# Order of the links of the down phase, and of two kinds of side work, in a fused attention and two-layer SiLU kernel

## The chip, the cores and the metric

The kernel runs on one core of a Trainium2 chip. The metric is the device time of one execution in microseconds (us), the median of several; lower is better. Engines are named as in the profile: PE (TensorE matmuls), PEld (TensorE weight loads), DVE (VectorE), ACT (ScalarE), POOL (GpSimd) and SP (SyncE, which issues nearly all DMAs).

## The reference

Three stages follow each other: an attention with a decay bias, a gated layer and a plain SiLU layer. The change lies in the last one, `_moe2_ref`, whose input is the 2304 x 512 result of the gated layer.

```python
def _moe_ref(x, w_gate, w_val, w_out):
    g = x @ w_gate
    silu = g * (1.0 / (1.0 + np.exp(-g)))
    val = x @ w_val
    return (silu * val @ w_out).astype(np.float32)

def _moe2_ref(x, w_in, w_out):            # x 2304 x 512, w_in 512 x 2048, w_out 2048 x 512
    h = x @ w_in
    g = h * (1.0 / (1.0 + np.exp(-h)))
    return (g @ w_out).astype(np.float32)

def reference(**kwargs):
    ...
    attn_out = _attn_ref(**attn_kwargs)
    B, H, S, D = attn_out.shape
    x = np.ascontiguousarray(attn_out.transpose(0, 2, 1, 3)).reshape(B * S, H * D)
    x = _moe_ref(x=x, **moe_kwargs)
    return _moe2_ref(x=x, **moe2_kwargs)
```

## The kernel before

**Matmuls in three parts.** Every fp32 operand is kept as a high part and a low part. A product is three matmuls: weight high by data high (L677 in the down phase), weight high by data low (L678), weight low by data high (L679). The up phase has L632, L635 and L636 for the same three. The high part of an intermediate is made by ACT (a copy, L112) and its low part by POOL (a subtraction, L609); the two together are `h_cut`. So L677 of a block needs ACT alone, and L678 behind it needs POOL.

**The last layer** runs from about 656 us to the end. Its tokens are taken in 3 groups of 768 (two halves of 384), its 2048 hidden columns in 8 pieces of 256, which makes 24 steps. Two steps, a = 2q and b = 2q + 1, and a down phase make a round q, 0 to 11; rounds 0 to 3 work on the first group of tokens, 4 to 7 on the second, 8 to 11 on the third. Both matrix products are written with seven block products in place of eight, so that sums and differences of blocks are operands too.

- `up2(i)` does the seven products of a step (the list UP, positions `("u", i, 0)` to `("u", i, 6)`), six matmuls each, into four PSUM banks of the pool `ps_m`. What comes out is made into SiLU values u0 to u3 and their differences t1 to t4.
- `down2(q)` does 14 links, `("d", q, 0)` to `("d", q, 13)`: the seven products X1 to X4, Y1, Y2, Z1, each once for step a (`e` = 0) and once for step b (`e` = 1). Each link is six matmuls, two output banks (m = 0, 1) by three. Chain X adds all its products up in the same two banks, chain Y in two others (pool `ps_o`), chain Z in two banks of `ps_m`. After each link of step b, DVE reads the chain's two banks into accumulators in SBUF (L114 the first time, L688 after it), and the next product of that chain may write them again only then. The operands are: X1 takes B11 (cut of u0), Y1 T1, X2 T2, Y2 B22 (cut of u3), X3 T3, Z1 B21 (cut of u2), X4 T4. X1, Z1 and X4 use one weight tile, named C; Y1, X2, X3 and Y2 another, named E.

**What sets the order.** All engines run in the order in which the code is written. `LINKS` gives the order of the links. `fill` is a table of side work: after position `at` of an up or down phase, the functions put there are written, on whichever engine they use. In it stand the `h_cut` of step a (in the up phase of b) and of step b (in the down phase), the differences `h_sub` on DVE (L614), the weight loads `u_load` on SP (L599), and the preparation of the next group's tokens: `x2_load` (L555) fetches them, `x2_sub` (L586) makes four differences t1 to t4 of them on DVE, in two halves each, and `x2_cut` makes the parts for matmuls on ACT (L112) and POOL (L565).

Of the kernel before, what the change touches and what calls it, by code (L numbers as in the profile page):

```python
# [43 lines left out]
    "Y1": ("T1", "E", 0, (1, 1)), "Y2": ("B22", "E", 3, (0, 1)), "Z1": ("B21", "C", 1, (0, 0)),  # L44
}
LINKS = [
    ("X1", 0), ("Y1", 0), ("X1", 1), ("Y1", 1), ("X2", 0), ("X2", 1), ("Y2", 0),
    ("Y2", 1), ("X3", 0), ("X3", 1), ("Z1", 0), ("Z1", 1), ("X4", 0), ("X4", 1),
]
CLOSED = ("Z1", "Y2", "X3", "X4")  # L50

# [15 lines left out]
def kernel(  # L67
# [42 lines left out]
    def copy(eng, out, in_, scale=1.0):  # L110
        if eng == "a":
            act_last[:] = [nc.scalar.activation(out=out, in_=in_, func=AF.Copy, scale=scale).ins]  # L112
        elif eng == "v":
            nc.vector.tensor_scalar(out=out, in0=in_, scalar1=scale, scalar2=None, op0=ALU.mult)  # L114
        else:
            nc.gpsimd.tensor_scalar(out=out, in0=in_, scalar1=scale, scalar2=1.0, op0=ALU.mult, op1=ALU.mult)
# [434 lines left out]
    def x2_load(t):  # L551
        for i in range(2):
            r = p2["x2", i] = p2["x2r"].tile([P, 2, 2, TN], F32, tag="x2r", name="x2r")
            src = x2_d[2 * i : 2 * i + 2, :, 2 * t * TN : 2 * (t + 1) * TN]
            nc.sync.dma_start(out=r, in_=src.rearrange("k p (h n) -> p k h n", h=2))  # L555
# [4 lines left out]
    def x2_cut(t, i, src=None, eng=nc.vector):  # L560
        x = p2["x", t, i] = p2["x2"].tile([P, 2, 2, TN], F32R, tag="x2", name="x2")
        if src is None:
            src = p2["x2", min(i, 1)][:, :, {0: 0, 2: 0, 5: 1}[i]]
        copy("a", x[:, 0], src)
        eng.tensor_tensor(out=x[:, 1], in0=src, in1=x[:, 0].bitcast(F32), op=ALU.subtract)  # L565

    def x2_sub(t, k, halves=(0, 1)):
        u, d = p2["x2", 0], p2["x2", 1]
        if 0 in halves:
            if t > 0:  # L570
                o = {1: None, 2: None, 3: u[:, :, 1], 4: u[:, :, 0]}[k]
                if o is None:
                    o = p2["st"].tile([P, 2 * TN], F32, tag="st", name="stage").rearrange("p (k n) -> p k n", k=2)
            else:
                if k % 2:
                    p2["tt"] = p2["x2"].tile([P, 2, 2, TN], F32, tag="x2", name="tt")
                o = p2["tt"][:, (k + 1) % 2]
            p2["t", k] = o
        a, b = {
            1: (u[:, :, 1], u[:, :, 0]), 2: (d[:, :, 1], p2.get(("t", 1))),  # L580
            3: (d[:, :, 1], u[:, :, 1]), 4: (d[:, :, 0], p2.get(("t", 2))),
        }[k]
        o = p2["t", k]
        if len(halves) == 1:
            o, a, b = [x[:, halves[0]] for x in (o, a, b)]
        nc.vector.tensor_tensor(out=o, in0=a, in1=b, op=ALU.subtract)  # L586

    def u_load(i, names):
        for name in names:
            wide = 768 if name in "ZC" else CW // 2  # L590
            if (i, name) == (1, "Z"):
                w = p2["x2"].tile([P, 2, wide], F32R, tag="x2", name="z1")
            elif name in "ZC" and i > 0 or name == "C":
                w = p2["wt2"].tile([P, 2, wide], F32R, tag="wt2", name="wt2")
            else:
                w = p2["wt"].tile([P, 2, CW // 2], F32R, tag="wt", name="wt")
            p2["w", i, name] = w
            src = wu_d[steps[i][1], "ZSCE".index(name), :, :, :wide]
            nc.sync.dma_start(out=w[:, :, :wide].bitcast(F32), in_=src)  # L599

    def part(i, name):
        p2["u", i, name] = p2["tmp"].tile([P, TN], F32, tag=name + str(i % 2) * (name in ("t3", "t4")), name=name)
        return p2["u", i, name]

    def h_cut(i, name, src):
        h = hs["2", i, name] = p2["h"].tile([P, 2, TN], F32R, tag="h2", name="h2")
        u = p2["u", i, src]
        copy("a", h[:, 0], u)
        nc.gpsimd.tensor_tensor(out=h[:, 1], in0=u, in1=h[:, 0].bitcast(F32), op=ALU.subtract)  # L609

    def h_sub(i, out, a, b):
        x, y = p2["u", i, a], p2["u", i, b]
        o = p2["u", i, out] if ("u", i, out) in p2 else part(i, out)
        nc.vector.tensor_tensor(out=o, in0=x, in1=y, op=ALU.subtract)  # L614
# [164 lines left out]
    def body():  # L779
# [57 lines left out]
        for c in range(last):  # L837
            b = batch[c]
            cur = chunk_steps(c)
            at = {k: [] for k in range(5)}  # L840
            if b + 1 < B:
                k, u0 = c % len(L1), (b + 1) * H
# [35 lines left out]
        for c in range(last, n1):  # L878
            cur = chunk_steps(c)
            k = c - last  # L880
# [4 lines left out]
            i = tail_pieces.get(c)  # L885
# [51 lines left out]
        def put(at, *f):  # L937
            fill.setdefault(at, []).extend(f)

        nq = len(steps) // 2  # L940
        for q in range(nq):
            a, b = 2 * q, 2 * q + 1
            put(("u", b, 0), lambda i=a: h_cut(i, "T1", "t1"), lambda i=a: h_cut(i, "T3", "t3"))
            put(("u", b, 0), lambda i=a: h_sub(i, "t2", "u3", "t1"))
            put(("u", b, 1), lambda i=a: h_cut(i, "B21", "u2"), lambda i=a: h_sub(i, "t4", "u2", "t2"))
            put(("u", b, 2), lambda i=a: h_cut(i, "T2", "t2"))
            put(("u", b, 6), lambda i=b: h_sub(i, "t2", "u3", "t1"), lambda i=a: h_cut(i, "T4", "t4"))
            put(("d", q, 0), lambda i=b: h_cut(i, "T1", "t1"), lambda i=b: h_sub(i, "t4", "u2", "t2"))
            put(("d", q, 1), lambda i=b: h_cut(i, "T2", "t2"))
            put(("d", q, 2), lambda i=b: h_cut(i, "T3", "t3"))  # L950
            put(("d", q, 3), lambda i=b: h_cut(i, "B21", "u2"))
            put(("d", q, 4), lambda i=b: h_cut(i, "T4", "t4"))
            if q > 0:
                put(("u", a, 0), lambda a=a: (u_load(a, "C"), u_load(a + 1, "C")))
                put(("u", a, 3), lambda a=a: (u_load(a, "E"), u_load(a + 1, "E")))
            else:
                put(("u", b, 0), lambda: u_load(1, "E"))
            if q + 1 < nq:
                put(("u", b, 1), lambda a=a: u_load(a + 2, "ZS"))
                put(("d", q, 0), lambda a=a: u_load(a + 3, "ZS"))  # L960
        for t in range(1, TG):
            q = 4 * t - 1
            put(("u", 2 * q - 5, 2), lambda t=t: x2_load(t))
            for at, x in (
                ((q - 1, 6), 0), ((q - 1, 7), 3), ((q - 1, 9), 1), ((q, 6), 4), ((q, 7), 2), ((q, 8), 5), ((q, 9), 6),
            ):
                src = {1: 1, 3: 2, 4: 3, 6: 4}.get(x)
                put(("d", *at), lambda t=t, x=x, k=src: x2_cut(t, x, p2["t", k] if k else None, nc.gpsimd))
            for e in range(2):
                for at, k in ((q - 3, 4), 1), ((q - 2, 4), 2), ((q - 1, 4), 3), ((q - 1, 10), 4):  # L970
                    put(("d", at[0], at[1] + 2 * e), lambda t=t, k=k, e=e: x2_sub(t, k, (e,)))
        for q in range(nq):
            up2(2 * q, fill)
# [3 lines left out]
        second_layer.close()  # L977

    body()


# [42 lines left out]
```

## Time and profile before

| | |
|---|---|
| median of 3 runs | 1030.31 us (1029.67 to 1032.68) |
| the profiled execution's own time | 1030.3 us |
| its span, first to last instruction | 1028.5 us |
| mean granted TensorE clock | 0.993 |
| busy in the span | PE 97%, PEld 90%, POOL 57%, DVE 57%, ACT 51% |
| DMA | 260 GB/s on average |

The time is device time, the span is what the trace covers; 1.8 us lie outside it. Busy shares are means over all stages. Matmuls overlap each other in the trace (in the last layer one lasts about 0.34 us and the next starts some 0.175 us after it), so a busy PE says less than the distance from one matmul's start to the next.

### The profile page before, as it was taken

Reading aid. Unit: us, or ns where it says so; the run is one execution under the profiler, and the core shown is the slowest. Engines: PE = TensorE matmul, PEld = TensorE weight load, DVE = VectorE, ACT = ScalarE, POOL = GpSimd, SP = SyncE. Lnnn points to the kernel's source line nnn. Section 1 sums busy time; section 2 is a strip of 40 time slices with the busy share of each in tenths; the row PEclk is TensorE's granted clock in tenths of the full one; section 3 lists DMA queues with packets and bytes.
Section 4 is the critical chain, followed back from the end, with each engine's and each line's share of the span. In section 5 each row is a group of like instructions: output and inputs, shape, how many; then the busy total and the mean of one; then the engine's idle time right before and its main releaser. Section 6 shows DMA issues by size and latency. Waiting matters only on the chain.

```text
span 1028.5 us, 19469 instructions
## 1 busy us (share of the span) xinstructions
PE 996.6 (97%) x6864; PEld 930.2 (90%) x6864; DVE 584.7 (57%) x1492; ACT 523.7 (51%) x1230; POOL 589.8 (57%) x757
## 2 busy tenths in 40 slices
PE   8789999999999999999999999999999999999998
PEld 5468898899898899899899999999999999999997
DVE  5877768635745645545632223356665657555555
ACT  6868878625665435655533543323554234544232
POOL 4767656615866646757542765435766447764445
PEclk8989999999999999999999999999999999999999
DMA  8679798758789799766767767885777855786652
GB/s 234 175 240 309 262 326 255 265 174 269 261 295 267 258 311 305 276 230 238 273 221 278 292 262 286 319 330 225 277 286 282 301 212 216 290 317 244 237 203 94
DMA packets 81617, 267.16 MB, mean 260 GB/s; under 512 B 9904, under 2 KB 29360, under 8 KB 66160
## 3 DMA queue, kind: packets, MB, share of 16 engines
q1 hardware_dynamic: 81376, 265.73, 74.1%
q8 instruction: 54, 0.88, 0.3%
q14 instruction: 43, 0.35, 0.1%
q10 hardware_dynamic: 144, 0.20, 0.1%
HBM read 208.15 MB, written 57.75 MB: 259 GB/s over the span
## 4 chain that ended last, share of the span: by engine, by line
PE 75%; POOL 6%; ACT 3%; DVE 3%; DMA 2%; issue 2%; POOLq 0%; SPq 0%; DVEq 0%; ACTq 0%
PE pgv L490 9%; PE pgv L492 9%; PE pgv L491 9%; POOL h L609 6%; PE po L490 5%; PE po L491 5%; PE po L492 5%; PE po L678 5%; PE po L679 4%; PE po L677 4%; PE pv L324 4%; PE pu L636 3%; PE pu L632 3%; PE pu L635 3%; PE psc L213 3%; PE ptr L283 3%
## 5 line engine op out<-in xcount | busy, mean ns | idle before, releaser
L490 PE MATMUL pgv<-xt,wt 128*128 128x288 f32 x768 | 229.5, 299 | 1.9 <-DVE wraw L388 1.9
L492 PE MATMUL pgv<-xt,wt 128*128 128x288 f32 x768 | 226.3, 295 | 0.0
L491 PE MATMUL pgv<-xt,wt 128*128 128x288 f32 x768 | 226.1, 294 | 0.0
L609 POOL TENSOR_TENSOR h<-u,h 128x384 fp32r<-128x384 f32 x72 | 74.5, 1034 | 156.4 <-ACT h L112 152.1
L490 PEld LDWEIGHTS pgv<-xt,wt 128*128 128x128 f32 x768 | 144.2, 188 | 12.8 <-DVE m L230 5.9
L492 PEld LDWEIGHTS pgv<-xt,wt 128*128 128x128 f32 x768 | 144.0, 188 | 0.2 <-issue 0.2
L491 PEld LDWEIGHTS pgv<-xt,wt 128*128 128x128 f32 x768 | 144.1, 188 | 0.0
L504 POOL TENSOR_TENSOR h<-u,h 128x288 fp32r<-128x288 f32 x96 | 79.5, 830 | 88.2 <-ACT h L112 84.3
L112 ACT ACTIVATE h<-u 128x288 fp32r<-128x288 f32 (+1 forms) x168 | 79.7, 475 | 97.8 <-DVE u L502 96.8
L678 PE MATMUL po<-h,wt 128*128 128x384 f32 x336 | 113.8, 339 | 10.5 <-POOL h L609 10.5
L490 PE MATMUL po<-h,wt 128*128 128x288 f32 x384 | 114.8, 299 | 0.0
L677 PE MATMUL po<-h,wt 128*128 128x384 f32 x336 | 112.7, 335 | 0.8 <-DVE acc L114 0.8
L491 PE MATMUL po<-h,wt 128*128 128x288 f32 x384 | 113.1, 295 | 0.0
L492 PE MATMUL po<-h,wt 128*128 128x288 f32 x384 | 113.0, 294 | 0.0
L679 PE MATMUL po<-h,wt 128*128 128x384 f32 x336 | 112.5, 335 | 0.0
L632 PE MATMUL pu<-x,wt 128*128 128x384 f32 x330 | 111.7, 339 | 0.0
L635 PE MATMUL pu<-x,wt 128*128 128x384 f32 x330 | 111.7, 339 | 0.0
L636 PE MATMUL pu<-x,wt 128*128 128x384 f32 x330 | 111.7, 339 | 0.0
L638 ACT ACTIVATE s<-pu 128x384 f32<-128x384 f32 x48 | 23.6, 492 | 172.7 <-PE pu L636 172.7
L609 POOL TENSOR_TENSOR h<-t,h 128x384 fp32r<-128x384 f32 x96 | 106.7, 1131 | 5.6 <-ACT h L112 4.6
L243 ACT ACTIVATE e<-e,m 64x64 f32<-64x64 f32 (+4 forms) x160 | 88.4, 554 | 33.9 <-DVE m L230 29.2
L688 DVE TENSOR_TENSOR acc<-po,acc 128x384 f32<-128x384 f32 x144 | 77.0, 556 | 50.0 <-PE po L679 49.9
(107 smaller groups left out, 2216.0 us busy)
## 6 DMA issues: line engine op xcount, KB each, us to landing
wt<-w_d SPq DMA_DIRECT2D x54, 1024.0 KB, 6.9
wt<-wu_d SPq DMA_DIRECT2D x48, 1024.0 KB, 9.0
wt<-wu_d SPq DMA_DIRECT2D x47, 768.0 KB, 6.5
r<-in_w_dram SPq DMA_DIRECT2D x36, 512.0 KB, 6.6
w_d<-wt SPq DMA_DIRECT2D x18, 1024.0 KB, 8.2
r<-in_w_dram SPq DMA_DIRECT2D x64, 256.0 KB, 7.4
qkr<-in_qk_dram SPq DMA_DIRECT2D x32, 288.0 KB, 7.8
cumb<-cum_d SPq DMA_DIRECT2D x15, 576.0 KB, 8.9
```

Of the source, the lines that this page charges most:

```text
L112: act_last[:] = [nc.scalar.activation(out=out, in_=in_, func=AF.Copy, scale=scale).ins]
L243: nc.scalar.activation(out=e[:r, hd, :wd], in_=e[:r, hd, :wd], func=AF.Exp, bias=m[hd][:r], scale=-1.0, accum_out=l[:r, hd : hd + 1],)
L490: nc.tensor.matmul(out=ps[:, :n], lhsT=a, rhs=xh, start=(k == 0), stop=False)
L491: nc.tensor.matmul(out=ps[:, :n], lhsT=a, rhs=xl, start=False, stop=False)
L492: nc.tensor.matmul(out=ps[:, :n], lhsT=c, rhs=xh, start=False, stop=(k == last))
L609: nc.gpsimd.tensor_tensor(out=h[:, 1], in0=u, in1=h[:, 0].bitcast(F32), op=ALU.subtract)
L632: nc.tensor.matmul(out=o, lhsT=a, rhs=x[:, 0, kk], start=fresh and kk == 0, stop=False, skip_group_check=True)
L635: nc.tensor.matmul(out=o, lhsT=a, rhs=x[:, 1, kk], stop=False, **more)
L636: nc.tensor.matmul(out=o, lhsT=c, rhs=x[:, 0, kk], stop=kk == 1, **more)
L677: nc.tensor.matmul(out=ps, lhsT=a, rhs=h[:, 0], start=fresh, stop=False, skip_group_check=True)
L678: nc.tensor.matmul(out=ps, lhsT=a, rhs=h[:, 1], stop=False, **more)
L679: nc.tensor.matmul(out=ps, lhsT=c, rhs=h[:, 0], stop=e == 1, **more)
```

## The change

Three things are moved, and no instruction is added or removed: the first step's Z1 goes from link 10 to link 2, so that seven links move back by one; the cut of T4 of step a goes from position 6 of step b's up phase to position 1 of the down phase, behind the cuts of T1 and T2 of step b; and the halves of the token differences of a group move (t1 from positions 4 and 6 to 11 and 13 of the same round, t2 and t3 from 4 and 6 to 5 and 7, t4 from 10 and 12 of a group's last round but one to 5 and 7 of its last).

```diff
 LINKS = [
-    ("X1", 0), ("Y1", 0), ("X1", 1), ("Y1", 1), ("X2", 0), ("X2", 1), ("Y2", 0),
-    ("Y2", 1), ("X3", 0), ("X3", 1), ("Z1", 0), ("Z1", 1), ("X4", 0), ("X4", 1),
+    ("X1", 0), ("Y1", 0), ("Z1", 0), ("X1", 1), ("Y1", 1), ("X2", 0), ("X2", 1),
+    ("Y2", 0), ("Y2", 1), ("X3", 0), ("X3", 1), ("Z1", 1), ("X4", 0), ("X4", 1),
 ]
...
-            put(("u", b, 6), lambda i=b: h_sub(i, "t2", "u3", "t1"), lambda i=a: h_cut(i, "T4", "t4"))
+            put(("u", b, 6), lambda i=b: h_sub(i, "t2", "u3", "t1"))
             put(("d", q, 0), lambda i=b: h_cut(i, "T1", "t1"), lambda i=b: h_sub(i, "t4", "u2", "t2"))
-            put(("d", q, 1), lambda i=b: h_cut(i, "T2", "t2"))
+            put(("d", q, 1), lambda i=b: h_cut(i, "T2", "t2"), lambda i=a: h_cut(i, "T4", "t4"))
...
             for e in range(2):
-                for at, k in ((q - 3, 4), 1), ((q - 2, 4), 2), ((q - 1, 4), 3), ((q - 1, 10), 4):
+                for at, k in ((q - 3, 11), 1), ((q - 2, 5), 2), ((q - 1, 5), 3), ((q, 5), 4):
                     put(("d", at[0], at[1] + 2 * e), lambda t=t, k=k, e=e: x2_sub(t, k, (e,)))
```

In the orders below, numbers behind names tell tiles apart; `po2` are the output banks, `h2` the cut operands, `wt2` and `wt` the weight tiles C and E.

PE, round 1, the second half of Y1 of step a and what follows it, before (`h2_9559` is B11 of step b, `h2_9599` its T1):

```order
L677 MATMUL po2_9612<-h2_9503,wt_9455 128x384
L678 MATMUL po2_9612<-h2_9503,wt_9455 128x384
L679 MATMUL po2_9612<-h2_9503,wt_9455 128x384
L677 MATMUL po2_9591<-h2_9559,wt2_9425 128x384
L678 MATMUL po2_9591<-h2_9559,wt2_9425 128x384
L679 MATMUL po2_9591<-h2_9559,wt2_9425 128x384
L677 MATMUL po2_9595<-h2_9559,wt2_9425 128x384
L678 MATMUL po2_9595<-h2_9559,wt2_9425 128x384
L679 MATMUL po2_9595<-h2_9559,wt2_9425 128x384
L677 MATMUL po2_9608<-h2_9599,wt_9457 128x384
L678 MATMUL po2_9608<-h2_9599,wt_9457 128x384
```

The same place of the changed kernel (`h2_9520` is B21 of step a, `h2_9559` again B11 of step b; T1 of step b comes after the rows shown):

```order
L677 MATMUL po2_9609<-h2_9503,wt_9455 128x384
L678 MATMUL po2_9609<-h2_9503,wt_9455 128x384
L679 MATMUL po2_9609<-h2_9503,wt_9455 128x384
L677 MATMUL po2_9619<-h2_9520,wt2_9423 128x384
L678 MATMUL po2_9619<-h2_9520,wt2_9423 128x384
L679 MATMUL po2_9619<-h2_9520,wt2_9423 128x384
L677 MATMUL po2_9623<-h2_9520,wt2_9423 128x384
L678 MATMUL po2_9623<-h2_9520,wt2_9423 128x384
L679 MATMUL po2_9623<-h2_9520,wt2_9423 128x384
L677 MATMUL po2_9588<-h2_9559,wt2_9425 128x384
L678 MATMUL po2_9588<-h2_9559,wt2_9425 128x384
```

Six matmuls of Z1 now stand between Y1 of step a and X1 of step b, and so ahead of Y1 of step b, whose L678 needs the low part of T1.

POOL, round 1, the low parts of the cuts around the start of the down phase, before (the name behind `<-` is the source; `t4_9523` is t4 of step a):

```order
L609 TENSOR_TENSOR h2_9571<-u3_9549,h2_9571 128x384
L609 TENSOR_TENSOR h2_9588<-t4_9523,h2_9588 128x384
L609 TENSOR_TENSOR h2_9599<-t1_9582,h2_9599 128x384
L609 TENSOR_TENSOR h2_9616<-t2_9586,h2_9616 128x384
L609 TENSOR_TENSOR h2_9627<-t3_9584,h2_9627 128x384
```

and in the changed kernel:

```order
L609 TENSOR_TENSOR h2_9571<-u3_9549,h2_9571 128x384
L609 TENSOR_TENSOR h2_9596<-t1_9582,h2_9596 128x384
L609 TENSOR_TENSOR h2_9613<-t2_9586,h2_9613 128x384
L609 TENSOR_TENSOR h2_9616<-t4_9523,h2_9616 128x384
L609 TENSOR_TENSOR h2_9627<-t3_9584,h2_9627 128x384
```

T4 of step a moves behind T1 and T2 of step b, on POOL and in the same way on ACT.

DVE, round 0, the readings of the output banks and the two halves of t1 (L586), before:

```order
L114 TENSOR_SCALAR acc2_9327<-po2_9299 128x384
L586 TENSOR_TENSOR stage_9341<-x2r_9224 128x384
L114 TENSOR_SCALAR acc2_9346<-po2_9278 128x384
L114 TENSOR_SCALAR acc2_9351<-po2_9282 128x384
L586 TENSOR_TENSOR stage_9341<-x2r_9224 128x384
L688 TENSOR_TENSOR acc2_9346<-po2_9295,acc2_9346 128x384
L688 TENSOR_TENSOR acc2_9351<-po2_9299,acc2_9351 128x384
```

and in the changed kernel:

```order
L688 TENSOR_TENSOR acc2_9325<-po2_9310,acc2_9325 128x384
L586 TENSOR_TENSOR stage_9395<-x2r_9224 128x384
L114 TENSOR_SCALAR acc2_9406<-po2_9275 128x384
L114 TENSOR_SCALAR acc2_9411<-po2_9279 128x384
L586 TENSOR_TENSOR stage_9395<-x2r_9224 128x384
L621 TENSOR_TENSOR w_9434<-pu_9427,s0_9421 128x384
```

The halves of t1, which read the fetched tokens `x2r`, now stand around the reading of the last product, X4, ahead of the next up phase (L621), and no longer ahead of the readings of X2 and Y2.

## Rows read from the trace of the kernel before

**Rows 1.** Page, part 1: busy us, share of the span, instructions.

```profile
PE 996.6 (97%) x6864; PEld 930.2 (90%) x6864; DVE 584.7 (57%) x1492; ACT 523.7 (51%) x1230; POOL 589.8 (57%) x757
```

**Rows 2.** Waits of PE, 660 to 1028 us: total, times, longest.

```profile
PE po L678 <- POOL h L609: 10.5, 12, 0.9
PE po L677 <- DVE acc L114: 0.8, 1, 0.8
```

**Rows 3.** Waits of PEld, the same stretch.

```profile
PEld po L678 <- POOL h L609: 14.3, 12, 1.2
PEld po L677 <- DVE acc L114: 1.1, 1, 1.1
```

**Rows 4.** Timeline of PE, round 4: start, duration, idle before and releaser.

```profile
794.38 0.34 PE L677 MATMUL po<-h,wt 128*128 128x384 f32 x1
...
797.53 0.34 PE L677 MATMUL po<-h,wt 128*128 128x384 f32 x1
798.74 0.44 PE L678 MATMUL po<-h,wt 128*128 128x384 f32 x1 [0.87 <-POOL h L609]
799.02 0.34 PE L679 MATMUL po<-h,wt 128*128 128x384 f32 x1
```

**Rows 5.** Chain that ended last, round 5: start, us, what.

```profile
829.35 0.44 PE po L678
```

**Rows 6.** Timeline of POOL, round 4, narrow windows.

```profile
791.48 1.01 POOL L609 TENSOR_TENSOR h<-u,h 128x384 fp32r<-128x384 f32 x1
...
796.08 1.34 POOL L609 TENSOR_TENSOR h<-t,h 128x384 fp32r<-128x384 f32 x1
...
797.39 1.30 POOL L609 TENSOR_TENSOR h<-t,h 128x384 fp32r<-128x384 f32 x1
...
800.60 1.32 POOL L609 TENSOR_TENSOR h<-u,h 128x384 fp32r<-128x384 f32 x1
801.88 1.01 POOL L609 TENSOR_TENSOR h<-t,h 128x384 fp32r<-128x384 f32 x1
```

**Rows 7.** Timeline of ACT, round 4.

```profile
795.29 0.94 ACT L112 ACTIVATE h<-t 128x384 fp32r<-128x384 f32 x2
796.58 0.94 ACT L112 ACTIVATE h<-t 128x384 fp32r<-128x384 f32 x2 [0.34 <-DVE t L614]
```

**Rows 8.** Timeline of DVE, round 4.

```profile
795.17 0.54 DVE L657 TENSOR_TENSOR t<-u,pu 128x384 f32<-128x384 f32 x1
795.63 2.20 DVE L614 TENSOR_TENSOR t<-u,t 128x384 f32<-128x384 f32 x2
...
799.40 1.08 DVE L114 TENSOR_SCALAR acc<-po 128x384 f32<-128x384 f32 x2 [0.63 <-PE po L679]
800.40 0.65 DVE L586 TENSOR_TENSOR stage<-x2r 128x384 f32<-128x384 f32 x1
```

**Rows 9.** Timeline of PE and DVE, round 0.

```profile
680.27 0.34 PE L679 MATMUL po<-h,wt 128*128 128x384 f32 x1
681.39 0.44 PE L677 MATMUL po<-h,wt 128*128 128x384 f32 x1 [0.78 <-DVE acc L114]
681.67 0.34 PE L678 MATMUL po<-h,wt 128*128 128x384 f32 x1
...
680.31 0.56 DVE L586 TENSOR_TENSOR stage<-x2r 128x384 f32<-128x384 f32 x1 [3.27 <-DMA x2r<-x_d]
```

**Rows 10.** Timeline of POOL and DVE, round 3 and the next up phase.

```profile
771.96 7.24 POOL L565 TENSOR_TENSOR x<-x2r,x 128x768 fp32r<-128x768 f32 x4
...
779.22 1.08 DVE L688 TENSOR_TENSOR acc<-po,acc 128x384 f32<-128x384 f32 x2 [1.00 <-PE po L679]
781.93 0.56 DVE L621 TENSOR_TENSOR w<-pu,s 128x384 f32<-128x384 f32 x1 [1.63 <-PE pu L636]
```

**Rows 11.** Windows, round 4: busy of each engine, clock, DMA share, GB/s.

```profile
807.00:808.50 1.50, 1.50 (x11) 1.50 (x10) 0.76 (x2) 0.00 (x0) 0.00 (x0) 1.00 0.00 0
```

**Rows 12.** Page, part 6: a weight load, KB and us to landing.

```profile
wt<-wu_d SPq DMA_DIRECT2D x48, 1024.0 KB, 9.0
```

## The prediction

> **What bounds the kernel now.** PE is busy 97% of the span [rows 1], so only PE's idle time can be won, unless work were taken from it, and none is. I therefore read the list of waits first, for the stretch of the last layer, since the order of instructions is the same before it. PE waits there for two things only: 12 times for the low part of an operand that POOL makes, 10.5 us in all and none over 0.9 us, and once for a reading of output banks by DVE, 0.8 us [rows 2]. Twelve is the number of rounds: the same wait once in each.
>
> The timeline of PE in round 4 shows where it stands. The down phase starts at 794.38; the 18 matmuls of its first three links take until 797.53, 0.175 us each; then the first matmul of Y1 of step b starts, and the second, the first to read the low part of T1, starts only at 798.74 [rows 4]. From start to start that is 1.21 us where 0.175 is usual, and the matmul behind it comes 0.28 us later instead of 0.175. So one stall costs 1.21 + 0.28 - 2 x 0.175 = 1.14 us. It comes back in round 5, where the chain of waits has the same L678 at 829.35 [rows 5], 30.61 us later: that is a round's time.
>
> What is late is read from POOL. It makes the low part of T4 of step a from 796.08 (1.34 us) and that of T1 of step b from 797.39 (1.30 us), that is until 798.69 [rows 6]; PE starts 0.05 us after it. POOL has no idle time ahead of T1: it is late because T4, which is wanted only by link 12, goes first. ACT made the high parts of both from 795.29 on, in 0.94 us [rows 7].
>
> The single DVE wait is in round 0. DVE reaches the first half of t1 (L586) and sits 3.27 us, until 680.31, for the tokens that the DMA brings; the bank readings behind it are late, and PE goes from 680.27 to 681.39 and on to 681.67 [rows 9]: 1.12 + 0.28 - 0.35 = 1.05 us.
>
> **The change part by part.**
>
> Z1 of step a at link 2. Its six matmuls are only moved. They put Y1 of step b 6 x 0.175 = 1.05 us later, so its L678 is wanted not at 797.53 + 0.175 = 797.70 but at 798.75. That alone would just meet 798.69. Can Z1 itself start at 794.38 + 2 x 1.05 = 796.48? Its weights are the tile C, which X1 has read two links before; the low part of B21 of step a ends at 791.48 + 1.01 = 792.49 [rows 6]; its two banks come from the pool of the up phase, and the last DVE operation that reads this phase's banks ends at 795.17 + 0.54 = 795.71 [rows 8]. So it waits for nothing, by 0.8 us. It now holds its banks nine links instead of one, but nothing else takes a bank of that pool in a down phase, and Z1 of step b, after which they come free, stays at link 11. Cost 0.
>
> T4 behind T1 and T2. T1 now has POOL's turn at 796.08, and ACT's first of the two at 795.29, done by about 795.8. Its low part ends at 796.08 + 1.34 = 797.42, 1.3 us ahead of 798.75. What follows: T2 takes T1's old turn and ends by 798.69, wanted by L678 of link 6 at 794.38 + 6 x 1.05 + 0.175 = 800.86. T4 of step a comes third and T3 fourth, where it was; T3 ends as B21 starts, about 800.60, wanted at 805.06. B21 (until 801.92) and T4 of step b (until 802.89) [rows 6] are wanted at 806.1 and 808.2, T4 of step a at 807.2. Each has 2 us or more, and POOL's and ACT's totals stay.
>
> The open cost here is POOL beside DVE. DVE runs two L614 in the 2.20 us from 795.63 [rows 8], and they share the stretch with T1's cut in its new turn; in the trace the cut in that very turn took 1.34 us against 1.01 elsewhere [rows 6], so I take 1.34. The far bound is that T1 waits until both L614 are through, at 797.83, and then needs 1.01: 798.84, and 798.89 at PE, 0.14 us too late, 12 x 0.14 = 1.7 us lost. The Trainium skill (SBUF — State Buffer, "Who interferes with whom") has a rule for this pair: DVE with two SBUF inputs and GpSimd lock each other out for a whole instruction, and the first to start wins. Read at its harshest it gives that far bound, 1.7 us; the trace, with 0.33 us of stretching, does not bear out so long a block.
>
> Seven links one place later. Each bank reading by DVE keeps its distance to the next writer of that bank, but for one: X3 of step b (now link 10) to X4 (link 12) has one link between instead of two. That is as close as X1 of step b to X2 of step a is, before and after, and there PE does not wait in any round. Cost 0, priced below as a rival.
>
> The token differences. Sixteen halves of 0.56 to 0.83 us move on DVE, none goes. t2 and t3 move with the readings they stand between: in round 4 such a half, 0.65 us at 800.40, comes straight behind the reading of 799.40, with time left to the next [rows 8]. t4's halves take the same kind of place in rounds 3 and 7. Who needs t4 there is the last of four token cuts; POOL runs these from 771.96 for 7.24 us, its last from about 777.4 [rows 10], while the second half is done by about 773. t1's halves come after link 11 and behind X4's reading, which ends at 780.30; DVE then idles 1.63 us before the next up phase wants it at 781.93 [rows 10], and 0.56 to 0.83 fits. In round 0, PE's start of 681.39 [rows 9] is that of link 8; without the stalls it would be 681.39 - 1.14 - 1.05 = 679.2, so link 11, behind which the first half now stands, ends some 4 x 1.05 later, about 683.4 us, 3 us after the tokens land. DVE no longer waits, and the 1.05 us are won. If the landing slipped past that, what stands behind is X4's reading, with a whole up phase to spare.
>
> Transfers. Nothing moves on SP's queue ahead of a weight load that was free to go. Rounds shorten by 1.14 of 30.61 us; DMA stands still late in each round (share 0.00 at 807 to 808.5 [rows 11]), since the loads wait for tiles, and a tile lands 9.0 us after issue [rows 12]. Cost 0; a late tile would show as PE waiting for a DMA, which it does nowhere here.
>
> **The sum.** 12 x 1.14 + 1.05 = 14.7 us. The profiled execution took 1030.3 us, the median of the runs is 1030.31, so no correction: 1030.3 - 14.7 = **1015.6 us**. Two other readings of the same stalls bound it: PE's listed idle time, 10.5 + 0.8 = 11.3 us [rows 2], gives 1019.0; the weight loads' idle time, 14.3 + 1.1 = 15.4 us [rows 3], gives 1014.9. Starts count what the next matmul loses too, so I take those. The far bound of POOL beside DVE would be 1017.3.
>
> **The rivals.**
>
> *Part of each stall stays*, because PE's slower pace after a restart or POOL beside DVE is not won back: 1017.3 to 1019.0. For it: POOL's 1.34 against 1.01 us. Against: a margin of 1.3 us.
>
> *The wait is not one for order.* Suppose T1 is late because its tile is not free; then it would stay late whatever goes before it, and only round 0's 1.05 us would be won: 1029.2, no change that counts. For it: the stall repeats with the same length in all rounds. Against: POOL goes from T4 to T1 without a pause [rows 6], so T1 was not held up by a reader of its tile. The Trainium skill (Perfetto Trace Analysis, "Optimization Strategy") holds that the same gap repeating on the engine that should be saturated can mean too few buffers; these rows speak against it.
>
> *Slower: X4 waits for DVE.* From the end of X3's last matmul into a bank to X4's first into it, the one link between leaves 10 x 0.175 - 0.34 = 1.4 us, and a reading needs half of 1.08, 0.54 us [rows 8], plus the way there, so some 0.8 us to spare. Only if DVE came more than 0.8 + 1.23 = 2.0 us late at that link in each round would the gain of 14.7 be eaten; at 2.3 us late a round costs 0.3 more than before and the kernel 1033.5. DVE sits idle 1.00 us ahead of such a reading [rows 10] and has no other work at link 10, so nothing speaks for it but the shorter distance.
>
> **How the numbers follow.** About 0.75 for the forecast (1014 to 1017.3), 0.17 for part of each stall staying (up to 1020), 0.05 for a wait that stays or comes up elsewhere with little gained, 0.03 for slower. The range that holds 8 in 10 and the bounds of the open costs is 1013.9 to 1019.4. About 0.3% (3 us) is what a measurement of this kernel can tell from no change: faster by more 0.93, within it 0.04, slower by more 0.03.
>
> **What would show it.** In the changed profile: no wait of PE for POOL's L609 in the last layer, and none for DVE in round 0; rounds of about 29.5 us; POOL's cut of T1 right behind that of B22, about 1.3 us sooner in its round; DVE not waiting for the tokens. The forecast is wrong if L678 of Y1 or X2 of step b still has idle time ahead of it, if an L677 of X4 waits for DVE, or if matmuls run at more than 0.175 us from start to start in the down phase.

## The result and the profile after

The changed kernel takes 1018.64 us, the median of 4 runs (1017.69 to 1020.24), against 1031.49 us for the kernel before in the same comparison: a ratio of 0.9871, interval 0.9836 to 0.9907. The forecast was 1015.6 us, with a range of 1013.9 to 1019.4.

The last layer does what the prediction said. PE's list of waits, which had the two rows of [rows 2] from 660 us on, has none there now. The two largest totals of the whole execution are of the attention stage (what waited for what, total us, times, longest):

```profile
PE ptr L283 <- POOL e L116: 6.2, 7, 2.1
PE ptr L289 <- DVE xt L339: 3.0, 3, 1.1
```

Timeline of PE in round 4 (start, duration), the answer to [rows 4]: the first matmul of the down phase, and the first three of Y1 of step b.

```profile
790.82 0.34 PE L677 MATMUL po<-h,wt 128*128 128x384 f32 x1
...
795.00 0.33 PE L677 MATMUL po<-h,wt 128*128 128x384 f32 x1
795.18 0.33 PE L678 MATMUL po<-h,wt 128*128 128x384 f32 x1
795.35 0.33 PE L679 MATMUL po<-h,wt 128*128 128x384 f32 x1
```

The 1.21 and 0.28 us between starts are now 0.18 and 0.17. L678 of Y1 comes 4.36 us after the phase's start, as it did in [rows 4] (798.74 - 794.38): the link of Z1 has filled the place of the stall.

Timelines of POOL and ACT in the same round, the answers to [rows 6, 7]:

```profile
791.53 1.02 POOL L609 TENSOR_TENSOR h<-u,h 128x384 fp32r<-128x384 f32 x1 [0.39 <-ACT h L112]
792.51 1.34 POOL L609 TENSOR_TENSOR h<-t,h 128x384 fp32r<-128x384 f32 x1
...
791.73 0.53 ACT L112 ACTIVATE h<-t 128x384 fp32r<-128x384 f32 x1
793.00 1.35 ACT L112 ACTIVATE h<-t 128x384 fp32r<-128x384 f32 x3 [0.75 <-DVE t L614]
```

POOL's cut behind B22 is now that of T1. It takes 1.34 us, as T4's did in this turn, and ends at 793.85; PE's L678 starts at 795.18, so 1.3 us are to spare. ACT makes T1's high part alone, waits for DVE, and then makes those of T2, T4 and T3.

Timeline of DVE in round 0, the answer to [rows 9]:

```profile
684.26 2.12 DVE L688 TENSOR_TENSOR acc<-po,acc 128x384 f32<-128x384 f32 x4 [1.00 <-PE po L679]
686.29 0.55 DVE L586 TENSOR_TENSOR stage<-x2r 128x384 f32<-128x384 f32 x1
687.38 1.08 DVE L114 TENSOR_SCALAR acc<-po 128x384 f32<-128x384 f32 x2 [0.54 <-PE po L679]
688.37 0.55 DVE L586 TENSOR_TENSOR stage<-x2r 128x384 f32<-128x384 f32 x1
```

The halves of t1 stand after the four readings of X3 and Z1 and after X4's; neither waits for the DMA.

How long the layer is can be read from PE's timeline. Before, its first matmul (L632) and its last are:

```profile
656.14 0.34 PE L632 MATMUL pu<-x,wt 128*128 128x384 f32 x1
...
1024.15 0.34 PE L679 MATMUL po<-h,wt 128*128 128x384 f32 x1
```

After, with the first L632 of two rounds that follow each other in between:

```profile
658.34 0.34 PE L632 MATMUL pu<-x,wt 128*128 128x384 f32 x1
...
717.12 0.34 PE L632 MATMUL pu<-x,wt 128*128 128x384 f32 x1
...
746.55 0.34 PE L632 MATMUL pu<-x,wt 128*128 128x384 f32 x1
...
1011.22 0.34 PE L679 MATMUL po<-h,wt 128*128 128x384 f32 x1
```

A round is 746.55 - 717.12 = 29.43 us, where it was 30.61. The layer is 1011.22 + 0.34 - 658.34 = 353.2 us; before it went from 656.14 to 1024.49, 368.35 us. That is 15.1 us less, yet the span fell by 12.9 only (1028.5 to 1015.6): the layer started 2.2 us later, though the change moves no instruction ahead of it. The time of these two executions fell by 12.6 us (1030.3 to 1017.69), since 2.1 us lie outside the span now and 1.8 did before. Windows of the first 100 us (busy time of each engine with its instructions, PE's granted clock, DMA share, GB/s) show what differs there. Before:

```profile
0.00:100.00 100.00, 84.41 (x581) 63.92 (x582) 75.08 (x274) 76.19 (x200) 64.17 (x132) 0.93 0.79 235
```

After:

```profile
0.00:100.00 100.00, 85.22 (x560) 64.11 (x561) 75.15 (x271) 74.06 (x196) 61.33 (x125) 0.90 0.78 226
```

In the same 100 us PE ran at a mean granted clock of 0.90 instead of 0.93, more of the time at the lower of its two levels (1.2 against 2.4 GHz), and got through 560 matmuls instead of 581. Whether this is the change's doing is tested below.

### The profile page after: what moved, and what is told of

It is laid out like the page before. It is cut to its first block, busy times and chain, and to the rows that moved or that the text cites. A ratio compares the mean times of both kernels' runs of the same rounds, so it can differ in the third digit from the quotient of the medians.

```text
span 1015.6 us, 19481 instructions
## 1 busy us (share of the span) xinstructions
PE 996.2 (98%) x6864; PEld 933.4 (92%) x6864; DVE 587.7 (58%) x1492; ACT 523.9 (52%) x1230; POOL 589.4 (58%) x757
## 4 chain that ended last, share of the span: by engine, by line
PE 90%; DVE 1%; ACT 0%; issue 0%; DVEq 0%
PE pgv L490 10%; PE pgv L492 9%; PE pgv L491 9%; PE pu L632 6%; PE pu L636 6%; PE pu L635 6%; PE po L677 6%; PE po L678 6%; PE po L679 6%; PE po L490 5%; PE po L491 5%; PE po L492 5%; PE pv L324 4%; PE psc L213 4%; PE ptr L283 3%; PE ptr L289 1%
## 5 line engine op out<-in xcount | busy, mean ns | idle before, releaser
L490 PEld LDWEIGHTS pgv<-xt,wt 128*128 128x128 f32 x768 | 144.7, 188 | 11.3 <-DVE m L230 5.9
L677 PE MATMUL po<-h,wt 128*128 128x384 f32 x336 | 112.4, 335 | 0.0
L678 PE MATMUL po<-h,wt 128*128 128x384 f32 x336 | 112.3, 334 | 0.0
L679 PE MATMUL po<-h,wt 128*128 128x384 f32 x336 | 112.3, 334 | 0.0
L632 PE MATMUL pu<-x,wt 128*128 128x384 f32 x330 | 111.7, 339 | 0.0
```

The source lines that it names most:

```text
L490: nc.tensor.matmul(out=ps[:, :n], lhsT=a, rhs=xh, start=(k == 0), stop=False)
L632: nc.tensor.matmul(out=o, lhsT=a, rhs=x[:, 0, kk], start=fresh and kk == 0, stop=False, skip_group_check=True)
L677: nc.tensor.matmul(out=ps, lhsT=a, rhs=h[:, 0], start=fresh, stop=False, skip_group_check=True)
L678: nc.tensor.matmul(out=ps, lhsT=a, rhs=h[:, 1], stop=False, **more)
L679: nc.tensor.matmul(out=ps, lhsT=c, rhs=h[:, 0], stop=e == 1, **more)
```

## The experiments

Since times of whole runs differ by some us, each kernel's last layer is measured from its trace, from the start of the first L632 to the end of the last L679.

| kernel | first L632 | last matmul's end | last layer, us |
|---|---|---|---|
| before | 656.14 | 1024.49 | 368.35 |
| before, another run | 659.39 | 1028.23 | 368.84 |
| changed | 658.34 | 1011.56 | 353.2 |
| changed, another run | 660.79 | 1014.10 | 353.3 |
| links alone | 660.24 | 1016.14 | 355.9 |
| T4's cut alone | 659.11 | 1014.81 | 355.7 |
| token differences alone | 656.47 | 1023.69 | 367.2 |
| links and T4's cut | 658.54 | 1012.64 | 354.1 |
| T4's cut and token differences | 660.23 | 1013.75 | 353.5 |
| links and token differences | 657.44 | 1012.51 | 355.1 |
| changed, T1 in the third turn | 659.04 | 1025.42 | 366.4 |
| changed, X4 right behind X3 | 659.53 | 1018.12 | 358.6 |

**Both kernels once more.** No edit.

> The changed kernel as it is, against the kernel before, on the same chip. By the theory the last layer, from its first matmul (L632) to the end of its last, is 353.2 us again within 0.2, and the ratio comes out near (1031 - 15)/1031 = 0.985. What moves the total by 1 to 3 us from run to run lies ahead of the last layer, where half-clock stretches of PE fall differently: its first L632 starts anywhere from 656 to 661 us. By the rival that the change itself made the earlier stages 2.2 us longer, the first L632 starts again within 0.3 us of 658.3.

> The kernel before as it is, one more look. By the theory the last layer is 368.35 us again within 0.2, with 12 stalls of 1.14 us, and the first L632 starts anywhere from 656 to 661 us (656.14 in the trace of before). By the rival that the changed kernel's earlier stages are longer, it starts within 0.3 us of 656.1 here, and at 658 or later only where the links or cuts are moved.

Changed against before: 1020.04 us (4 runs) against 1034.21 (7 runs), ratio 0.9859, interval 0.9842 to 0.9875. The layers are 353.3 and 368.84 us; the second is 0.5 us over the first trace of before, not within 0.2. About half of that is round 0's longer DVE wait, 1.0 us instead of the 0.8 of [rows 2]; the rest is an L632 ahead of it that starts 0.25 us late, with a late matmul behind it. PE's waits from 660 us on in the second run of before:

```profile
PE po L678 <- POOL h L609: 10.3, 12, 0.9
PE po L677 <- DVE acc L114: 1.0, 1, 1.0
```

The layer of before starts at 659.39 us here, later than that of the changed kernel in its first trace (658.34), and its window of the first 100 us is:

```profile
0.00:100.00 100.00, 84.80 (x561) 62.93 (x562) 74.16 (x271) 74.12 (x196) 61.54 (x126) 0.91 0.75 227
```

561 matmuls at a clock of 0.91: the unchanged kernel has the slow first stage too, so a late start does not need the change. The starts of all kernels spread from 656.1 to 660.8 us; the three lowest (before, token differences alone, links and token differences) are the three runs that got through 581 matmuls in their first 100 us, the others through 550 to 563. The clock does not sort them by itself: X4 right behind X3 had 0.93, as the three had, and got through 563. What makes the first stage differ is left open.

Most runs of the two kernels have no trace, but a span on record. Taking off 368.6 and 353.3 us for the last layer gives an estimate of what lies outside it: 659.8 to 664.9 us before (17 runs, middle one 663.6), 662.3 to 665.2 us with the change (8 runs, middle 664.1). The middle values are half a us apart, within a spread of 3 to 5 us, so the later start of the first trace is not shown to be the change's doing. What does differ in every run is the time outside the span: 2.1 to 2.2 us in the 8 runs of the changed kernel, 1.7 to 1.9 in the 17 of before. Of the variants below only the two that have both T4's cut and the token differences moved show as much (T4's cut and token differences; X4 right behind X3); why is left open.

**The links alone.**

```diff
 LINKS = [
-    ("X1", 0), ("Y1", 0), ("X1", 1), ("Y1", 1), ...
+    ("X1", 0), ("Y1", 0), ("Z1", 0), ("X1", 1), ("Y1", 1), ...
```

> Kernel before with the new list of links alone; T4 of step a still goes through POOL ahead of T1, and the token differences stay. By the theory of order (what counts is when PE wants T1's low part against when POOL's turn comes), the link of Z1 moves the want from 797.70 to 798.75 in round 4 and POOL is done at 798.69, with PE 0.05 us behind it: a stall of 0 to 0.1 us a round where 1.14 was, so 12.5 to 13.7 us are won, and round 0 keeps its 1.05 us wait for DVE. By the rival that the two moves add up (each brings a part of the stall), about half, 7 us, is won. By the rival of a tile that is not free, POOL would be no sooner and the stall gone all the same, with POOL showing idle time ahead of T1.

1019.77 us, ratio 0.9873 (0.9852 to 0.9893); the layer is 12.45 us shorter, at the low end of what was expected. PE's timeline in round 4:

```profile
798.51 0.34 PE L677 MATMUL po<-h,wt 128*128 128x384 f32 x1
798.70 0.44 PE L678 MATMUL po<-h,wt 128*128 128x384 f32 x1
798.98 0.34 PE L679 MATMUL po<-h,wt 128*128 128x384 f32 x1
```

T1's low part arrives just when PE wants it. No idle time of PE is listed for L678, but it lasts 0.44 us and the next start comes 0.28 us later: the 0.1 us of a slow restart without a wait of PE ahead of it. The weight loads do list it:

```profile
PEld po L678 <- POOL h L609: 2.1, 12, 0.2
```

The rival of two halves is out: this move alone takes nearly all.

**T4's cut alone.**

```diff
-            put(("u", b, 6), lambda i=b: h_sub(i, "t2", "u3", "t1"), lambda i=a: h_cut(i, "T4", "t4"))
+            put(("u", b, 6), lambda i=b: h_sub(i, "t2", "u3", "t1"))
...
-            put(("d", q, 1), lambda i=b: h_cut(i, "T2", "t2"))
+            put(("d", q, 1), lambda i=b: h_cut(i, "T2", "t2"), lambda i=a: h_cut(i, "T4", "t4"))
```

> Kernel before with the cut of T4 alone moved behind T1 and T2; links and token differences stay. By the theory of order T1's low part is done at 796.08 + 1.34 = 797.42 in round 4 and wanted at 797.70: no stall, 13.7 us won, round 0 keeps its 1.05 us. If DVE and POOL block each other for whole instructions there, T1 is done at 798.84 and nothing is won. If the tile was not free, POOL is idle ahead of T1 and nothing is won either. If the two moves add up, about half is won, 7 us.

1019.19 us, ratio 0.9865 (0.9832 to 0.9897); the layer is 12.7 us shorter, where 13.7 were expected. The 12 waits for POOL are gone altogether. PE's waits from 640 us on:

```profile
PE po L677 <- DVE acc L114: 1.6, 1, 1.6
PE pu L632 <- DMA wt<-wu_d: 0.3, 1, 0.3
```

The two rows make up the difference. Round 0's wait did not keep its size but grew from 0.8 to 1.6 us idle: the tokens land 24.4 us after the layer's start (24.2 before), and PE, without its stall, comes sooner to the bank that DVE has not read. The second row is a weight tile that lands late, 8.3 us into the layer. The same L632 starts late, by less than 0.05 to 0.4 us, in other runs too, among them the second runs of both kernels.

**The token differences alone**, and **the other two without them.**

```diff
-                for at, k in ((q - 3, 4), 1), ((q - 2, 4), 2), ((q - 1, 4), 3), ((q - 1, 10), 4):
+                for at, k in ((q - 3, 11), 1), ((q - 2, 5), 2), ((q - 1, 5), 3), ((q, 5), 4):
```

> Kernel before with the token differences alone moved. By the theory only round 0's wait of DVE for the fetched tokens goes: PE's 12 stalls of 1.14 us stay, its wait for DVE (0.8 us idle, 1.05 from start to start) goes, and the last layer is 1.05 us shorter. Rival: the halves of t4 and t1 in their new places delay bank readings or the next up phase, and PE shows new waits for DVE or ACT in rounds 3, 4, 7 or 8.

> Changed kernel with the token differences back in their old places. By the theory the 12 stalls stay away and round 0's wait comes back, now on the link after the one of before, at about 1.1 us from start to start; no other wait of PE in the last layer. Rival: the moves of t2, t3 and t4 were needed to keep the later links free of waits, and PE waits for DVE in several rounds.

One run each. Alone they shorten the layer by 1.1 us: the 12 waits for POOL stay, the one for DVE is gone. PE's waits with the token differences alone:

```profile
PE po L678 <- POOL h L609: 10.5, 12, 0.9
```

Taken out of the changed kernel, they leave 354.1 us, 0.9 more than with them, and this one wait:

```profile
PE po L677 <- DVE acc L114: 0.6, 1, 0.6
```

So neither t4's new place nor those of t2 and t3 do or cost anything that PE feels; t1's is worth 0.9 to 1.1 us.

**Each of the first two moves with the token differences.**

> The kernel before with the cut of T4 and the token differences moved, and the links as before. By the theory the links are not needed: T1's low part is done about 0.3 us before PE wants it, round 0's wait for DVE is gone, PE waits for nothing in the last layer, and it is as long as that of the changed kernel, 353.2 us within 0.2, or 0.6 more where a weight tile lands late in round 0 as in other runs. By the rival that the links bring something of their own, it is 354.4 us or more (0.1 us a round).

> The changed kernel with the cut of T4 back ahead of T1 on ACT and POOL; links and token differences as in the changed kernel. By the theory PE reaches Y1 of step b just as T1's low part is done: no listed idle time, but 0.28 instead of 0.175 us to the next matmul, 0.1 us in each of 12 rounds, so the last layer is 354.4 to 354.8 us. By the rival that the order of the cuts does not matter once the link is moved, 353.2 us.

One run each, no further edit. Without the links the layer is 353.5 us, with none of the 12 stalls; the 0.3 us over the changed kernel is one late L677 in round 0, for which the weight loads name ACT's high part. Without T4's move it is 355.1 us, 0.3 over the expected band, of which 0.15 are a late start ahead of round 0, and the weight loads show the 12 slow restarts:

```profile
PEld po L678 <- POOL h L609: 2.1, 12, 0.2
```

**T1 in the third turn.** Two cuts ahead of T1 where before had one: in the changed kernel T4 and T2 go ahead of it on ACT and POOL.

```diff
-            put(("u", b, 6), lambda i=b: h_sub(i, "t2", "u3", "t1"))
-            put(("d", q, 0), lambda i=b: h_cut(i, "T1", "t1"), lambda i=b: h_sub(i, "t4", "u2", "t2"))
-            put(("d", q, 1), lambda i=b: h_cut(i, "T2", "t2"), lambda i=a: h_cut(i, "T4", "t4"))
+            put(("u", b, 6), lambda i=b: h_sub(i, "t2", "u3", "t1"), lambda i=a: h_cut(i, "T4", "t4"))
+            put(("d", q, 0), lambda i=b: h_cut(i, "T2", "t2"), lambda i=b: h_sub(i, "t4", "u2", "t2"))
+            put(("d", q, 1), lambda i=b: h_cut(i, "T1", "t1"))
```

> The changed kernel, but the cuts at the start of the down phase in the order T4 of step a, T2, T1 of step b, so that T1 has POOL's third turn instead of its first. By the theory of order T1's low part, done two turns later, ends near 799.75 on round 4's clock of before and is wanted at 798.75: a stall of 1.0 us and 0.1 for the slow restart in each of 12 rounds, 13 us in all, last layer about 366.4 us. By the rival that PE's want alone had counted (the link of Z1 is what won the time), the order of the cuts costs less than 3 us.

One run: 1031.21 us, layer 366.38 us, 13.2 us longer than the changed kernel's. PE's timeline in round 4:

```profile
800.15 0.34 PE L677 MATMUL po<-h,wt 128*128 128x384 f32 x1
801.29 0.45 PE L678 MATMUL po<-h,wt 128*128 128x384 f32 x1 [0.81 <-POOL h L609]
801.58 0.34 PE L679 MATMUL po<-h,wt 128*128 128x384 f32 x1
```

From start to start 1.14 and 0.29 us, a stall of 1.08 us in each round. Same links, same instructions, and the stall is back at the size that POOL's turn against PE's want gives: some 13 us were expected, 13.2 came.

**X4 right behind X3.** The price of the rival for slower: Z1 of step b goes ahead of X3 of step b.

```diff
-    ("Y2", 0), ("Y2", 1), ("X3", 0), ("X3", 1), ("Z1", 1), ("X4", 0), ("X4", 1),
+    ("Y2", 0), ("Y2", 1), ("X3", 0), ("Z1", 1), ("X3", 1), ("X4", 0), ("X4", 1),
```

> The changed kernel with Z1 of step b ahead of X3 of step b, so that no link lies between X3 of step b and X4, which writes the same two banks. By the theory X4's first matmul comes 4 x 0.175 - 0.34 = 0.36 us after the end of X3's last into that bank, and the reading needs 0.54 and some 0.05 us: a wait of 0.2 to 0.3 and a slow restart of 0.1 us in each round, so 4 to 5 us for the kernel, last layer 357 to 358.5 us, PE waiting for DVE at L677. By the rival that DVE's readings are far from the path, nothing: 353.2 us.

One run: 1024.26 us, layer 358.6 us, 0.1 over the expected band. Timeline of PE at X4 in round 4, and then the wait of the weight loads from 640 us on:

```profile
806.42 0.34 PE L679 MATMUL po<-h,wt 128*128 128x384 f32 x1
806.89 0.45 PE L677 MATMUL po<-h,wt 128*128 128x384 f32 x1
807.17 0.34 PE L678 MATMUL po<-h,wt 128*128 128x384 f32 x1
```

```profile
PEld po L677 <- DVE acc L688: 5.3, 12, 0.4
```

0.47 + 0.28 - 0.35 = 0.40 us in each of 12 rounds, 4.8 us; 0.5 of the 5.4 us are the late weight tile. So DVE's reading is on the path when no link lies between, as priced, and off it with one.

## Why the prediction was right, and what it mis-sized

**What bounds.** Right. PE's 13 stalls were all its waits in the last layer, and with them gone PE goes from one matmul to the next without a gap over 0.2 us from 658 us to its end.

**Z1 at link 2, T4 behind T1 and T2.** Each step's times came out as worked out: T1's cut 1.34 us in its new turn, 1.3 us ahead of PE's want; the link's move by itself would "just meet" T1, which the run with the links alone shows, to the 0.1 us of a restart. What the prediction did not say, though its own numbers did, is that T4's move would do by itself: 797.42 against 797.70 is in time. The experiments show the two as two ways to the same gain, not two parts of it: of the 12 stalls (12 x 1.18 = 14.2 us) T4's move alone takes all, and the links alone take all but the restarts (1.7 us). In the changed kernel the link is spare room of 1.05 us, and costs nothing.

**POOL beside DVE.** The near value, 1.34 us, was right, not the far bound that T1 waits out both L614. The Trainium skill's rule (SBUF — State Buffer, "Who interferes with whom") fits the trace when it is read instruction by instruction: the cut loses time to one L614, 0.33 us, and each L614 stands behind one cut (0.91 us the first, 1.19 the second), so that the pair takes 2.20 us where a DVE operation of that size takes 0.54 [rows 8]. That it is this lock was not tried by itself.

**The token differences.** Right: 1.05 us foreseen, 0.9 to 1.1 measured, round 0 alone.

**The sum.** The stalls were worth 15.1 us (15.5 between the two later runs), not 14.7. A round lost 1.18 us, not 1.14: after a restart the next few matmuls come slightly late too (in round 4 of before nine starts behind it take 1.59 us, nine later ones 1.56). PE's listed idle time (11.3 us) was far off; the weight loads' (15.4 us) came as near as the sum of starts.

**The base.** What mis-sized the total is "so no correction": the forecast was made against one execution whose first stage was a quick one. Other runs of the same kernel go up to 1035.7 us (with that one its median became 1031.49), and its layer begins at 656.1 us in one trace and at 659.4 in the other. Of the 15.1 us won in the layer, a start 2.2 us later and the 0.3 us outside the span left 12.6 in the first pair of executions; the medians of the second comparison lie 14.2 apart. So the first median came out 3.0 us over the forecast. That it still fell into the range is partly luck: the changed kernel's second median, 1020.04, lies above the range's end of 1019.4.

**The rivals.** That part of each stall stays is what links alone show (0.1 us a round), and did not happen with T4 moved. That the tile was not free is refuted: with as many tiles as before, T1's cut starts straight behind B22's in the changed kernel, and the stall comes back when T1 gets the third turn. X4 waiting for DVE is real but needs the link between to go.

## What to carry to other kernels

When PE waits for an operand, look at what its maker does just before it: here an operation that is wanted nine links later stood ahead of it in the queue, and moving that back by two places was worth as much as rearranging PE's own order. Price a stall from start to start of the matmuls around it, not by the idle time listed. Measure such an edit on the stage in which it acts, since the rest of the run can move by several us by itself.

## What the runs showed of the hardware

A matmul that is released just in time, with no wait listed for PE, is still followed by a late one: 0.28 us to the next start instead of 0.175, in every round of the run with the links alone. What the trace shows beside it is the weight load: in round 4 of that run the weight load of L678 waits 0.17 us for POOL and starts together with its matmul, at 798.70; in the changed kernel it starts at 795.01, 0.17 us ahead of its matmul. That this is the reason was not tried by itself. With the matmuls behind it a restart comes to some 0.14 us: the layer without T4's move is 355.1 - 353.2 - 0.15 = 1.7 us longer, over 12 restarts.

The granted clock in the first 100 us was 0.88 to 0.93 from run to run, of programs that are the same up to there, and PE got through 550 to 581 matmuls in them.
